# q's short-row loads on GpSimd's queue, the attention's steps for a pair laid singly, and k^T v two steps later in unit 2

## The chip, the cores and the metric

The kernel runs on one core of one Trainium2 chip. Its time is the device time of one launch in microseconds (us); the time before is a median of three runs. The profile is one further execution of the same program (span 956.1 us), recorded with its instructions, their waits and every DMA packet.

## The reference, cut to what matters

```python
# q, k, v: (8 batches, 8 heads, 576 rows, 64), float32
kv  = einsum('bhsd,bhse->bhde', k, v)            # k^T v, per batch and head
out = einsum('bhsd,bhde->bhse', q, kv)
rms = sqrt(mean(out * out, axis=-1) + 1e-6)
att = out / rms * g_norm                          # -> x: (4608 tokens, 512)
h = x @ w_in                                      # (4608, 2048)
r = maximum(h, 0)
y = (s * (r * r) + b) @ w_out                     # (4608, 512)
```

The attention is linear: all of k and v of a batch is folded into eight 64x64 matrices first, and each row of q only multiplies one of them. Nearly all arithmetic is in the two matrix products of the feed-forward block.

## The kernel before, in words

**Units and chunks.** The 4608 tokens are 36 chunks of 128 rows, and four chunks are a unit: nine units, `u = 0` to `8`, in one Python loop that is fully laid out. ("Unit 2" below is `u == 2`, the third of them.) A unit's feed-forward block has two parts. `mm1(u, s)` makes the hidden activations in four steps `s = 0..3`, each of seven products of a Strassen-like scheme, `x1, x3, z2, y4, x6, y7, x5` (`x3` and `y4` are those of the step before). `mm2(u)` multiplies by w_out; for `u > 1` it uses a second level of the same scheme, in the function `rest`, and its w_out blocks come from DRAM again for each unit.

**The order is written by hand** (`manual_schedule`): every engine executes its instructions in the order of the Python calls, and semaphores are put in where data need them. So an instruction that must wait holds up all that stands behind it on its engine, and a DMA that must wait holds up all DMAs behind it in the same issuing queue.

**Attention on the side.** While unit `u` is in its feed-forward block, the attention of unit `u + 1` is laid between its products by `sides(u)` (for `u = 0` and `1` by `side_of(u)`). Two pairs of chunks, A and B, pass through these steps: `turn` (VectorE transposes q), `product` (TensorE multiplies by k^T v, and VectorE turns the result back out of PSUM), `square` (ScalarE), `row_sum` (VectorE and a root on ScalarE), `norm` (VectorE), `turn_x` (VectorE), `scale` (ScalarE), and at the end `x_sums` (VectorE). The dictionary `first` maps a place `(s, n)` to the steps laid there: `n = 0` before `x1`, `1` after `z2` (and before `y4`), `2` after `x6`, `3` after `y7`. `second` holds places in `rest`, called by `at(...)`.

**k^T v.** `kv_product(b)` makes the matrices of batch b with 144 small matmuls. It reads k and v from four tiles of a ring of seven (`ringp`), which also carries all w_out blocks. `pump(k)` issues the next k loads of one long list (`queue_w2`) on SyncE's queue, lines L115 (k and v), L779 and L782 (w_out): a load waits until all that used the ring slot seven places earlier is done. In unit 1 the function `parts_of_w(i)` also writes second-level parts of w_out to DRAM: seven DMAs for each of six blocks, from GpSimd's queue (L826), three of them straight out of the ring tiles, so that those stores too must have landed before their slots can be loaded again.

**q.** A pair's q is one 128x1024 tile; the pool `qp` has two buffers, so a pair's load waits for the `norm` of the pair two before it. From chunk 9 on q is loaded by `load_q` in DMAs of one head and half of its 64 columns: 32 rows of n runs of 128 bytes, 16 DMAs for each contiguous stretch of the batch. In the kernel before all of them are issued from SyncE's queue, where the ring's loads are. The profile names them by the caller: L1341 in `loads`, which issues a whole pair, and L1352 in `loads_in_parts`, which spreads a pair over eight places of unit 1's second part. Output rows leave by GpSimd's queue (L914).

**parts.** `parts(c)` says which rows of which batch chunk c holds; `store` uses the same table, so any choice gives the same output. A chunk in the middle of a group of nine takes half its rows from each of two batches.

Of the kernel before, what the change touches and what calls it, by code (L numbers as in the profile page):

```python
# [16 lines left out]
def kernel(  # L17
# [39 lines left out]
    nc = tc.nc  # L57
    P = 128
    B, H, S, D = q.shape
# [10 lines left out]
    U = CH // 4  # L70
# [23 lines left out]
    kv_in, q_in, q_tile, w_raw = {}, {}, {}, {}  # L94
# [25 lines left out]
    def parts(c):  # L120

        g, i = divmod(c, R)
        n = 1 if g == 0 else 2
        if i == 4:
            return [(2 * g, 8 * n, n), (2 * g + 1, 8 * n, n)]
        b, i = (2 * g, i) if i < 4 else (2 * g + 1, i - 5)
        return [(b, i, 1), (b, 4 + i, 1)] if g == 0 else [(b, 4 * i, 4)]

    def load_q(c, queues=(nc.sync, nc.sync)):

        t = qp.tile([P, 2 * DM], FP32, name="q_sb", tag="q")
        q_tile[c] = t
        pieces = []
        for i in range(2):
            if c + i < R:
                q_in[c + i] = t[:, i * DM : i * DM + DM].rearrange("p (h d) -> p h d", h=H)
        for s, queue in enumerate(queues):
            for i in range(2):  # L140
                if c + i < R:
                    b, j, _ = parts(c + i)[s]
                    queue.dma_start(
                        out=q_in[c + i][s * HB : s * HB + HB],
                        in_=q[b].rearrange("h (p j) d -> p j h d", j=R)[:, j],
                    )
        for i in range(2):
            if c + i < R:
                continue
            w = 4 * i  # L150
            for b, j, n in parts(c + i):
                if pieces and pieces[-1][1] == b and pieces[-1][2] + pieces[-1][3] == j:
                    pieces[-1][3] += n
                else:
                    pieces.append([w, b, j, n])
                w += n
            q_in[c + i] = t.rearrange("p (a w) -> p a w", a=NP)[:, :, i * P : i * P + P]
            if c + i == R:
                q_in[R] = t[:, DM:].rearrange("p (a w) -> p a w", a=NP)
        rest = []  # L160
        for w, b, j, n in pieces:
            src = q[b].rearrange("h (t j) d -> h t j d", j=JC)
            to = t.rearrange("p (a w d) -> p a w d", a=NP, d=32)
            if c < R:
                to, w = t[:, DM:].rearrange("p (a w d) -> p a w d", a=NP, d=32), 0
            for h in range(H):
                for a in range(2):
                    rows = slice(32 * (2 * (h % 2) + a), 32 * (2 * (h % 2) + a) + 32)
                    rest.append(
                        partial(  # L170
                            nc.sync.dma_start,
                            out=to[rows, h // 2, w : w + n, :],
                            in_=src[h, :, j : j + n, a * 32 : a * 32 + 32],
                        )
                    )
        return rest
# [160 lines left out]
    for h in range(H):  # L337
        e = D // KC
        nc.gpsimd.dma_start(
            out=g_col[h * e : h * e + e, :], in_=g_norm.rearrange("(e c) -> e c", c=KC)  # L340
# [159 lines left out]
    def attention_of_two(c):  # L500
# [5 lines left out]
        u, j = divmod(c, 4)  # L506
        by_block = []
        for i in range(2):
            p = parts(c + i)
# [7 lines left out]
        W = 8  # L517
        st = {}
# [20 lines left out]
        def product():  # L539
            ps = [ps_t.tile([P, 2, 2 * P], FP32, name="y_ps", tag="t") for _ in range(2)]  # L540
            for b, lo, hi in runs:
                for r in range(2):
                    for p in range(NP):
                        for l in range(2):
                            rows = slice(l * HB, l * HB + HB)
                            at = l * HB + r * 32
                            nc.tensor.matmul(  # L547
                                ps[l][32 * p : 32 * p + 32, r, lo:hi],
                                lhsT=bd_kv[b % 2][rows, p, at : at + 32],
                                rhs=st["qT"][rows, p, lo:hi],  # L550
                                start=True,
                                stop=True,
                            )
            st["y"] = q_tile[c].rearrange("p (w l d) -> p w l d", w=W, l=2)
            for l in range(2):
                nc.vector.transpose(
                    out=st["y"][:, :, l].rearrange("p w (r e) -> p r w e", r=2),
                    in_=ps[l].rearrange("p r (w t) -> p r w t", w=W),
                )

        def square():
# [22 lines left out]
        def turn_x():  # L584
# [6 lines left out]
            )  # L591

        return dict(
            turn=turn, product=product, square=square, row_sum=row_sum, norm=norm,
            turn_x=turn_x, scale=lambda: scale_x(u, j),
        )

# [708 lines left out]
    def side_of(u):  # L1306

        A, B = pairs_of(u + 1)
        sums = lambda: [fn() for fn in x_sums(u + 1)]
        if u == 0:  # L1310
            side = {
                6: [lambda: kv_product(1)],
                7: [partial(A["turn"], 0), partial(A["turn"], 1)],
                8: [A["product"], A["square"]],
                9: [A["row_sum"], partial(B["turn"], 0), partial(B["turn"], 1)],
                10: [A["norm"], A["turn_x"], A["scale"], B["product"], B["square"]],
                11: [B["row_sum"], B["norm"]],
                12: [B["turn_x"], B["scale"], lambda: [fn() for fn in sums_w_in(0)]],
                13: [sums],
            }  # L1320
        else:
            side = {
                2: [partial(A["turn"], 0), partial(A["turn"], 1)],
                4: [A["product"], A["square"]],
                5: [A["row_sum"], B["turn"]],
                6: [A["norm"]],
                7: [A["turn_x"], A["scale"], B["product"], B["square"]],
                8: [B["row_sum"]],
                9: [B["norm"]],
                11: [B["turn_x"], B["scale"]],  # L1330
                12: [sums],
            }
            for n, fn in enumerate(loads_in_parts(3, 0, 8)):
                side.setdefault(6 + n, []).append(fn)
        return side

    def loads(u, i):

        if u < U:
            for load in load_q(4 * u + 2 * i):  # L1340
                load()  # L1341

    def loads_in_parts(u, i, parts):

        left = []

        def part(n):
            if n == 0 and u < U:
                left.extend(load_q(4 * u + 2 * i))
            k = -(-len(left) // (parts - n))  # L1350
            for load in left[:k]:
                load()  # L1352
            del left[:k]

        return [partial(part, n) for n in range(parts)]


    tile_at = {1: 3, 2: 4, 3: 5, 4: 6, 5: 7, 6: 8, 7: 9, 9: 10, 10: 11, 11: 12, 12: 13, 14: 14, 15: 15}
    more_at = {8: 8, 9: 9, 12: 10, 13: 11, 14: 12, 15: 13}
# [19 lines left out]
    def sides(u):  # L1379

        first, second = {}, {}
        if u + 1 < U:
            A, B = pairs_of(u + 1)
        kv = [lambda: kv_product(kv_due[u]), lambda: pump(NP)] if u in kv_due else []
        q = {half: [partial(loads, u + 2, half)] for half in range(2)}
        if u == 1:
            for s in range(1, NS):
                first[((0, 1), (0, 3), (1, 1))[s - 1]] = list(sums_w_in(s))  # L1390
            first[1, 3] = kv + [partial(loads, 2, 1)]
            return first, second
        if u + 1 == U:
            return first, second
        soon = u == 2
        first = {
            (0, 1): [A["turn"], *(kv if soon else [])],
            (0, 3): [A["product"]],
            (1, 0): [A["square"]],
            (1, 1): [*([] if soon else kv), A["row_sum"]],  # L1400
            (1, 2): [A["norm"], B["turn"]],
            (1, 3): q[0],
            (2, 0): [A["turn_x"], A["scale"]],
            (2, 1): [B["product"]],
            (2, 2): [B["square"]],
            (2, 3): [B["row_sum"]],
            (3, 0): [B["norm"]],
            (3, 1): [B["turn_x"], *q[1]],
            (3, 2): [B["scale"]],
        }  # L1410
        second[5], second[6] = [[lambda n=n: x_sums(u + 1)[n]()] for n in range(2)]
        return first, second

    for u in range(U):
        if u == 0:
            first_unit()
            second = mm2(0)
        else:
            if u < 3:
                loads(u + 1, u - 1)  # L1420
            steps = [mm1(u, s) for s in range(NS)]
            first, at_second = sides(u)
            second = mm2(u, steps[-1], at_second) if u > 1 else mm2(u)
# [81 lines left out]
```

## Time and profile before

| what | value |
|---|---|
| time before, median of 3 | 958.62 us (958.38 to 960.95) |
| profiled execution, span | 956.1 us |
| TensorE busy / VectorE / ScalarE / GpSimd | 922.4 / 670.8 / 197.0 / 87.8 us |
| DMA moved | 165.80 MB, mean 173 GB/s |
| q loads from SyncE with rows of 128 bytes | 304 DMAs |

TensorE is busy for 96% of the span. Its instructions overlap a little, so busy time alone doesn't say what is lost; the places where it stands still, and the clock that it is granted there, do. A table of stretches, one per unit, and the order of time on single engines are the views that answer that. In all of them "L" is the line of the kernel before, "SPq" and "POOL" are the queues of SyncE and GpSimd, and "idle before <-" names what ended an engine's wait.

### The profile page before, as it was taken

Reading aid. Unit: us, or ns where it says so; the run is one execution under the profiler, and the core shown is the slowest. Engines: PE = TensorE matmul, PEld = TensorE weight load, DVE = VectorE, ACT = ScalarE, POOL = GpSimd, SP = SyncE. Lnnn points to the kernel's source line nnn. Section 1 sums busy time; section 2 is a strip of 40 time slices with the busy share of each in tenths; the row PEclk is TensorE's granted clock in tenths of the full one; section 3 lists DMA queues with packets and bytes.
Section 4 is the critical chain, followed back from the end, with each engine's and each line's share of the span. In section 5 each row is a group of like instructions: output and inputs, shape, how many; then the busy total and the mean of one; then the engine's idle time right before and its main releaser. Section 6 shows DMA issues by size and latency. Waiting matters only on the chain.

```text
span 956.1 us, 17631 instructions
## 1 busy us (share of the span) xinstructions
PE 922.4 (96%) x7118; PEld 830.4 (87%) x7118; DVE 670.8 (70%) x1175; ACT 197.0 (21%) x355; POOL 87.8 (9%) x170
## 2 busy tenths in 40 slices
PE   7999999999589999979999999999999999999997
PEld 6888888888478998879988998899889988998897
DVE  2789777587357776765767776787587768774685
ACT  2684132101023102220123003300230023001200
POOL 2000010053300002000300020003000110011000
PEclk9999999999799999998999999999999999999999
DMA  9588837478852586137831784178516810682075
GB/s 234 197 315 242 268 90 207 113 237 289 256 150 38 172 257 226 24 83 240 267 104 23 266 274 134 21 232 261 178 29 204 285 61 1 201 286 65 12 229 168
DMA packets 129568, 165.80 MB, mean 173 GB/s; under 512 B 78160, under 2 KB 85072, under 8 KB 129360
## 3 DMA queue, kind: packets, MB, share of 16 engines
q1 hardware_dynamic: 118256, 142.71, 49.3%
q0 software_dynamic: 7488, 19.41, 6.1%
q10 hardware_dynamic: 3744, 2.56, 1.1%
q8 instruction: 56, 0.92, 0.4%
q14 instruction: 24, 0.20, 0.1%
HBM read 136.84 MB, written 27.79 MB: 172 GB/s over the span
## 4 chain that ended last, share of the span: by engine, by line
PE 81%; DVE 6%; SPq 6%; DMA 3%; ACT 3%; issue 1%; ACTq 0%; DVEq 0%
PE x_ps L91 36%; PE y_ps L91 25%; PE z_ps L91 9%; PE t_ps L91 8%; SPq L1341 2%; SPq L1352 2%; PE kv_ps L378 2%; DVE a L248 1%; PE y_ps L547 1%; DMA w_raw<-in_moe_w_in_dram 1%; ACT r L688 1%; SPq L115 1%; ACT xT L498 1%; DVE a L643 1%; DMA kv_sb<-in_k_dram 1%
## 5 line engine op out<-in xcount | busy, mean ns | idle before, releaser
L688 ACT COPY r<-x_ps 128x512 f32<-128x512 f32 x96 | 55.9, 583 | 466.4 <-PE x_ps L91 392.6
L91 PE MATMUL x_ps<-xs,ws 128*128 128x256 f32 x512 | 124.2, 386 | 2.2 <-ACT r L688 2.2
L91 PE MATMUL y_ps<-xs,wb 128*128 128x256 f32 x512 | 122.0, 381 | 0.0
L914 POOL DMA_DIRECT2D out_dram<-o x110 | 54.5, 502 | 711.3 <-DVE o L248 552.6
L91 PEld LDWEIGHTS x_ps<-xs,ws 128*128 128x128 f32 x512 | 96.8, 192 | 20.4 <-ACT r L688 4.6
L91 PEld LDWEIGHTS y_ps<-xs,wb 128*128 128x128 f32 x512 | 96.1, 190 | 14.5 <-issue 1.7
L91 PE MATMUL x_ps<-xT,wa 128*128 128x256 f32 x384 | 89.6, 380 | 0.1
L248 DVE TENSOR_TENSOR a<-y_ps,r 128x512 f32<-128x512 f32 x64 | 43.7, 683 | 59.8 <-ACT r L688 46.5
L91 PEld LDWEIGHTS x_ps<-xT,wa 128*128 128x128 f32 x384 | 72.3, 190 | 10.2 <-ACT xT L498 0.5
L91 PE MATMUL y_ps<-w_sb,sub 128*128 128x128 f32 x560 | 69.4, 275 | 0.0
L91 PEld LDWEIGHTS y_ps<-w_sb,sub 128*128 128x128 f32 x560 | 66.4, 192 | 0.4
L91 PE MATMUL x_ps<-w_sb,s 128*128 128x256 f32 x256 | 61.0, 394 | 5.7 <-DMA w_sb<-w 5.7
L643 DVE SCALAR_TENSOR_TENSOR a<-a 128x512 f32<-128x512 f32 x89 | 61.5, 691 | 2.8
L91 PE MATMUL y_ps<-w_sb,a 128*128 128x128 f32 (+1 forms) x416 | 61.0, 295 | 0.0
L91 PEld LDWEIGHTS x_ps<-w_sb,s 128*128 128x128 f32 x256 | 49.6, 199 | 13.0 <-issue 6.3
L91 PE MATMUL x_ps<-xT,ws 128*128 128x256 f32 x256 | 60.5, 379 | 0.0
L91 PE MATMUL z_ps<-xT,wa 128*128 128x256 f32 x256 | 60.5, 379 | 0.0
L91 PEld LDWEIGHTS y_ps<-w_sb,a 128*128 128x128 f32 x416 | 55.5, 192 | 2.0
L91 PE MATMUL t_ps<-w_sb,sub 128*128 128x128 f32 x448 | 54.6, 275 | 0.0
L91 PEld LDWEIGHTS z_ps<-xT,wa 128*128 128x128 f32 x256 | 48.6, 190 | 6.6
L91 PEld LDWEIGHTS x_ps<-xT,ws 128*128 128x128 f32 x256 | 48.1, 190 | 6.2
L91 PEld LDWEIGHTS t_ps<-w_sb,sub 128*128 128x128 f32 x448 | 52.3, 192 | 0.0
(159 smaller groups left out, 1357.3 us busy)
## 6 DMA issues: line engine op xcount, KB each, us to landing
w_sb<-w SPq DMA_DIRECT2D x154, 512.0 KB, 4.8
w_sb<-w SPq DMA_DIRECT2D x42, 256.0 KB, 3.6
w_raw<-in_moe_w_in_dram SPq DMA_DIRECT2D x8, 1024.0 KB, 7.7
w_raw<-in_moe_w_out_dram SPq DMA_DIRECT2D x8, 1024.0 KB, 5.3
w_sb<-in_k_dram SPq DMA_DIRECT2D x48, 144.0 KB, 3.6
w_sb<-in_v_dram SPq DMA_DIRECT2D x48, 144.0 KB, 4.0
w<-sub POOLq DMA_DIRECT2D x24, 256.0 KB, 5.6
out_dram<-o POOLq DMA_DIRECT2D x92, 64.0 KB, 4.4
```

Source lines behind the costliest of these rows:

```text
L91: nc.tensor.matmul(o, lhsT=lhsT, rhs=rhs, start=start, stop=stop, skip_group_check=True)
L115: nc.sync.dma_start(out=kv_in[b, n][r * HB : r * HB + HB, m], in_=src[b, NP * r + n].rearrange("(p j) d -> p j d", j=R),)
L248: nc.vector.tensor_tensor(out=o, in0=a, in1=b, op=ALU.add)
L378: nc.tensor.matmul(ps[r][l * HB : l * HB + HB, i, :], lhsT=kv[l][rows, 0, j, :], rhs=kv[l][rows, 1, j, :], start=(j == 0), stop=(j == R - 1),)
L498: nc.scalar.activation(to[:, i], to[:, i], AF.Copy, scale=g_col[:, i : i + 1])
L547: nc.tensor.matmul(ps[l][32 * p : 32 * p + 32, r, lo:hi], lhsT=bd_kv[b % 2][rows, p, at : at + 32], rhs=st["qT"][rows, p, lo:hi], start=Tr ...
L643: nc.vector.scalar_tensor_tensor(t, t, 0.0, t, ALU.max, ALU.mult)
L688: nc.scalar.copy(st[name], src)
L914: queues[s % 2].dma_start(out=view[b, jj, :, cols], in_=st[name, j][s * w : s * w + w, cols])
L1341: load()
L1352: load()
```

## The change

Three edits go together.

1. The DMAs of q in short rows are issued from GpSimd's queue. With that, `loads_in_parts` goes: in unit 1 the pairs of unit 2 are loaded whole at the start of the unit, and those of unit 3 whole after the two `norm` steps of its second part (places 6 and 9).
2. `product` is cut in two, `product` (TensorE) and `back` (VectorE's transposes out of PSUM), and the steps of both pairs are spread so that most places hold one. In unit 2 they stand later: `kv_product` goes from place (0, 1) to (1, 1), `product` of A from (0, 3) to (1, 3), and B's last steps move into `rest`.
3. `parts(c)` takes the rows of the middle chunk from the start of the second batch instead of its end, which makes some stretches contiguous: the pair at chunk 22 needs 32 DMAs instead of 48.

```diff
     def parts(c):
         g, i = divmod(c, R)
-        n = 1 if g == 0 else 2
+        if g == 0:
+            if i == 4:
+                return [(0, 8, 1), (1, 8, 1)]
+            b, i = (0, i) if i < 4 else (1, i - 5)
+            return [(b, i, 1), (b, 4 + i, 1)]
         if i == 4:
-            return [(2 * g, 8 * n, n), (2 * g + 1, 8 * n, n)]
-        b, i = (2 * g, i) if i < 4 else (2 * g + 1, i - 5)
-        return [(b, i, 1), (b, 4 + i, 1)] if g == 0 else [(b, 4 * i, 4)]
+            return [(2 * g, 16, 2), (2 * g + 1, 0, 2)]
+        return [(2 * g, 4 * i, 4)] if i < 4 else [(2 * g + 1, 4 * i - 18, 4)]
...
-                            nc.sync.dma_start,
+                            nc.gpsimd.dma_start,
                             out=to[rows, h // 2, w : w + n, :],
...
-            st["y"] = q_tile[c].rearrange("p (w l d) -> p w l d", w=W, l=2)
+            st["ps"] = ps
+
+        def back():
+            y = q_tile[c].rearrange("p (w l d) -> p w l d", w=W, l=2)
             for l in range(2):
                 nc.vector.transpose(
...
-                6: [A["norm"]],
+                6: [A["norm"], partial(loads, 3, 0)],
...
-                9: [B["norm"]],
+                9: [B["norm"], partial(loads, 3, 1)],
...
-            for n, fn in enumerate(loads_in_parts(3, 0, 8)):
-                side.setdefault(6 + n, []).append(fn)
...
-            first[1, 3] = kv + [partial(loads, 2, 1)]
+            first[1, 3] = kv
...
-        soon = u == 2
-        first = {
-            (0, 1): [A["turn"], *(kv if soon else [])],
-            (0, 3): [A["product"]],
-            (1, 0): [A["square"]],
-            (1, 1): [*([] if soon else kv), A["row_sum"]],
-            (1, 2): [A["norm"], B["turn"]],
-            (1, 3): q[0],
-            (2, 0): [A["turn_x"], A["scale"]],
-            (2, 1): [B["product"]],
-            (2, 2): [B["square"]],
-            (2, 3): [B["row_sum"]],
-            (3, 0): [B["norm"]],
-            (3, 1): [B["turn_x"], *q[1]],
-            (3, 2): [B["scale"]],
-        }
+        if u == 2:
+            first = {
+                (0, 2): [A["turn"]],
+                (1, 1): kv,
+                (1, 3): [A["product"]],
+                (2, 0): [A["back"]],
+                (2, 1): [A["square"]],
+                (2, 2): [A["row_sum"], B["turn"]],
+                (2, 3): [B["product"]],
+                (3, 0): [B["back"]],
+                (3, 1): [A["norm"]],
+                (3, 2): [A["turn_x"], *q[0]],
+                (3, 3): [B["square"]],
+            }
+            second = {
+                0: [A["scale"]], 3: [B["row_sum"]], "norm": [B["norm"]],
+                4: [B["turn_x"], B["scale"], *q[1]],
+            }
+        else:
+            first = {
+                (0, 2): [A["turn"]],
+                (0, 3): [A["product"]],
+                (1, 0): [A["back"]],
+                (1, 1): [A["square"], *kv],
+                (1, 2): [A["row_sum"]],
+                (1, 3): [B["turn"]],
+                (2, 0): [A["norm"]],
+                (2, 1): [B["product"], *q[0]],
+                (2, 2): [A["turn_x"], B["back"]],
+                (2, 3): [B["square"]],
+                (3, 0): [A["scale"], B["row_sum"]],
+                (3, 1): [B["norm"]],
+                (3, 2): [B["turn_x"], *q[1]],
+            }
+            second = {0: [B["scale"]]}
...
-            if u < 3:
-                loads(u + 1, u - 1)
+            if u == 1:
+                loads(2, 0)
+                loads(2, 1)
```

More of the change, by code (lines that the diff above doesn't have):

```diff
@@ L553, in product @@
                             )
-            st["y"] = q_tile[c].rearrange("p (w l d) -> p w l d", w=W, l=2)
+            st["ps"] = ps
+        def back():
+            y = q_tile[c].rearrange("p (w l d) -> p w l d", w=W, l=2)
             for l in range(2):
                 nc.vector.transpose(
-                    out=st["y"][:, :, l].rearrange("p w (r e) -> p r w e", r=2),
-                    in_=ps[l].rearrange("p r (w t) -> p r w t", w=W),
+                    out=y[:, :, l].rearrange("p w (r e) -> p r w e", r=2),
+                    in_=st["ps"][l].rearrange("p r (w t) -> p r w t", w=W),
                 )
@@ L593, in attention_of_two @@
         return dict(
-            turn=turn, product=product, square=square, row_sum=row_sum, norm=norm,
+            turn=turn, product=product, back=back, square=square, row_sum=row_sum, norm=norm,
             turn_x=turn_x, scale=lambda: scale_x(u, j),
@@ L1313, in side_of @@
                 7: [partial(A["turn"], 0), partial(A["turn"], 1)],
-                8: [A["product"], A["square"]],
+                8: [A["product"], A["back"], A["square"]],
                 9: [A["row_sum"], partial(B["turn"], 0), partial(B["turn"], 1)],
-                10: [A["norm"], A["turn_x"], A["scale"], B["product"], B["square"]],
+                10: [A["norm"], A["turn_x"], A["scale"], B["product"], B["back"], B["square"]],
                 11: [B["row_sum"], B["norm"]],
@@ L1323, in side_of @@
                 2: [partial(A["turn"], 0), partial(A["turn"], 1)],
-                4: [A["product"], A["square"]],
+                4: [A["product"], A["back"], A["square"]],
                 5: [A["row_sum"], B["turn"]],
-                6: [A["norm"]],
-                7: [A["turn_x"], A["scale"], B["product"], B["square"]],
+                6: [A["norm"], partial(loads, 3, 0)],
+                7: [A["turn_x"], A["scale"], B["product"], B["back"], B["square"]],
                 8: [B["row_sum"]],
-                9: [B["norm"]],
+                9: [B["norm"], partial(loads, 3, 1)],
                 11: [B["turn_x"], B["scale"]],
@@ L1341, in loads @@
                 load()
[L1343 to L1355, printed above, removed]
     tile_at = {1: 3, 2: 4, 3: 5, 4: 6, 5: 7, 6: 8, 7: 9, 9: 10, 10: 11, 11: 12, 12: 13, 14: 14, 15: 15}
```

## The prediction

> **What bounds the kernel now.** I read the page's first two parts, then a table of stretches cut at each unit's first matmul, then the order of time on TensorE where a unit is longer than its neighbours, then on SyncE's queue just ahead of it.
>
> ```profile
> PE 922.4 (96%) x7118; PEld 830.4 (87%) x7118; DVE 670.8 (70%) x1175; ACT 197.0 (21%) x355; POOL 87.8 (9%) x170
> ```
>
> TensorE is the bound, and little is left outside it. The stretches of units 2 to 6 (columns: length, then busy time of PE, PEld, DVE, ACT, POOL, granted clock, DMA share, GB/s):
>
> ```profile
> 243.13:358.53 115.40, 102.09 (x834) 92.56 (x833) 73.92 (x134) 17.83 (x35) 7.28 (x13) 0.94 0.58 167
> 358.53:466.11 107.58, 101.44 (x801) 91.42 (x801) 73.10 (x134) 17.84 (x35) 6.90 (x14) 0.97 0.51 158
> 466.11:564.72 98.61, 98.34 (x834) 89.60 (x833) 73.02 (x134) 17.84 (x35) 6.54 (x14) 1.00 0.55 167
> 564.72:663.32 98.60, 98.23 (x833) 89.59 (x833) 73.01 (x134) 17.84 (x35) 9.17 (x19) 1.00 0.56 169
> 663.32:761.92 98.60, 98.34 (x833) 89.78 (x833) 73.00 (x134) 17.84 (x35) 7.83 (x16) 1.00 0.57 173
> ```
>
> With the same work, units 4 to 6 take 98.60 us, unit 2 takes 115.40 and unit 3 107.58. The excess, 16.8 + 9.0 = 25.8 us, comes with a clock below 1.00. TensorE in order of time (start, length, and in brackets the idle time before):
>
> ```profile
> 246.67 1.37 PE L378 MATMUL kv_ps<-w_sb 64*64 64x64 f32 x74
> 249.16 0.30 PE L378 MATMUL kv_ps<-w_sb 64*64 64x64 f32 x2 [1.12 <-DMA w_sb<-in_v_dram]
> 257.81 0.47 PE L378 MATMUL kv_ps<-w_sb 64*64 64x64 f32 x2 [8.35 <-DMA w_sb<-in_v_dram]
> 259.08 2.15 PE L378 MATMUL kv_ps<-w_sb 64*64 64x64 f32 x66 [0.80 <-DMA w_sb<-in_v_dram]
> 261.16 3.68 PE L91 MATMUL x_ps<-xs,ws 128*128 128x256 f32 x8
> 269.19 1.36 PE L547 MATMUL y_ps<-qT,bd_kv 64*32 64x192 f32 x64 [2.62 <-DVE qT L526]
> ...
> 429.13 6.73 PE L91 MATMUL x_ps<-w_sb,s 128*128 128x256 f32 x16 [5.71 <-DMA w_sb<-w]
> ```
>
> Unit 2: `kv_product` runs from 246.67 to 261.16, 14.5 us where its row elsewhere takes 2.5: 12.0 lost. The next eight matmuls take 3.5 us to the next start, not 1.73: 1.8 lost. Then 2.62 us for q's transpose. Together 16.4. Unit 3: 5.71 us for a w_out block, then 16 matmuls in 6.73 us where the same row takes 3.46 elsewhere: 9.0. Each time SyncE's queue was busy with q:
>
> ```profile
> 242.64 11.01 SPq L1352 DMA_DIRECT2D q_sb<-in_q_dram  x8
> 253.81 1.11 SPq L115 DMA_DIRECT2D w_sb<-in_k_dram  x2
> 254.97 1.23 SPq L115 DMA_DIRECT2D w_sb<-in_v_dram  x2
> ...
> 380.93 43.50 SPq L1341 DMA_DIRECT2D q_sb<-in_q_dram  x64
> 424.54 0.38 SPq L779 DMA_DIRECT2D w_sb<-w  x1
> ```
>
> The last k and v tile of unit 2 was issued only at 253.81, behind eight q loads; in unit 3 no w_out block was issued for 43.5 us, behind 64 of them; units 4 and 5, with 48 q loads in 36.4 and 35.2 us, lost nothing. So it is the length of the block in SyncE's queue, against the time until the ring runs dry, that decides.
>
> **What the Trainium skill says.** "DMA: Bandwidth & Descriptors", section Issuing engines are not separate DMA queues: issuing from several engines "will only save the time on the sequencer". The trace agrees on what that can be worth: those 64 DMAs move 1 MB in 43.5 us, so the queue was the limit there, not the DMA engines. "TensorE: Matmul & The Clock Gate", section What's actually happening: after an idle window of about 3.4 us the clock is halved. The trace agrees (5.71 us idle, then 6.73 for 3.46). "Perfetto Trace Analysis", section DMA Instruction — SWDGE (GPSIMD): the recorded end of a GpSimd DMA is its last descriptor, not the data. The trace agrees: L826's stores take 0.546 us and land 5.6 us after issue. "SBUF — State Buffer", section Who interferes with whom: VectorE's copies in the two-port mode lock GpSimd out; unit 1 has none in the stretch below, and L826's stores take 540 to 555 ns beside VectorE's busy stretches as elsewhere.
>
> **The change part by part.**
>
> *Unit 3.* Its q loads leave SyncE, so the block for `x5_of(0)` is issued when its slot is free, as in unit 4. `parts` takes 16 of 64 DMAs away. Removes 9.0 us. On GpSimd 48 loads at 0.6 us are 29 us of a queue that has nothing else until the stores at the unit's end. Hidden. The same for units 4 to 7, where no wait was lost to this.
>
> *Unit 2, the price.* GpSimd now has a queue in unit 1 that matters. In order: `parts_of_w(7)`, 32 loads for chunk 12, 16 for chunk 14 (after B's `norm`, done at 231.9), two output stores, `parts_of_w(3)`. The last k and v tile of unit 2 takes the ring slot of block (3, 0), whose first store out of the ring is the first DMA of `parts_of_w(3)`. That this kind of wait binds shows at 227.80: SyncE waits 1.8 us for such a store with the first of the four tiles. So behind the 48 loads stands that store, behind it the tile, behind that TensorE. The trace has no q load on GpSimd. Nearest rows there: 502 ns (L914, 32 rows), 546 (L826 from sub, 128 rows), 764 (L826 out of the ring, 512 runs of 512 bytes), a slope of about 0.57 ns per run. The loads have 192, 64 and 256 runs: 0.59, 0.52 and 0.63 us, 16 of each, 27.8 us. Lower end 0.50 each, 24.0. Upper end 0.76 each, 36.5, by the 764 ns row; I also get about that if loads land in 6 us (as SyncE's did at 222 to 232) and eight are in flight, which is how the kernel's ninth GpSimd DMA, 2.80 us held for the first one's landing, reads.
>
> From the trace: GpSimd ends `parts_of_w(7)` at 223.0; +1.6, as the first loads wait for those stores to land; +27.8; +1.06 for two output stores; +0.76 for the ring store; +3.3 to land (the median of L826 at 193 to 200, a quiet stretch; about 6 in a busy one). That is 257.5. The tile needed 5.3 us from issue to the matmul before (253.81 to 259.08): ready at 262.8. TensorE comes to the place later than before: (1, 1) is after eight products, 243.13 + 8 x 1.73 = 257.0, and the first half of `kv_product` takes 1.25: 258.2. Wait: 4.6 us, and being over the idle window, 3.3 us at half clock as in unit 3. So 16.4 goes and 7.9 comes. The 2.62 us for q's transpose goes: q of chunk 12 is issued by about 243, and `turn` comes at (0, 2), about 248.
>
> *Laid singly.* In units 2 to 7 TensorE waits once each, 0.3 to 0.4 us (2.2 in all), for ScalarE's copy r, which waits for VectorE's add, which stands behind the transposes out of PSUM at (2, 1), 1.31 us. Now `back` stands after `y4`'s add. But at (3, 1) a `norm` of 1.46 us stands before that add where a transpose of 1.24 stood, with about 0.2 us to spare. I take half: 1.1 gained. In unit 2's `rest` VectorE gets 1.22 + 1.46 + 1.24 us more, in a stretch where it is busy about 18.6 of 23.2 us: it fits, nearly; 0.7 lost, between 0 and 2.
>
> *Units 0 and 1, the tail.* The order on TensorE stays. Unit 1 starts with 32 loads on GpSimd, from 144 to about 163, wanted at 195 and 216: hidden. Nothing moves in unit 8.
>
> Sum: 958.6 - 16.4 + 7.9 - 9.0 - 1.1 + 0.7 = 940.7.
>
> **The rivals.** (a) No wait is left in unit 2: at 0.50 us a load and landing in 3.3, the store lands at 253.7 and the tile is ready at 259.0, a wait under 1 us and no halved clock. For it: L914's short stores do 0.50. Against: more runs per DMA cost more in L826. 958.6 - 16.4 - 9.0 - 1.1 + 0.7 = 932.8. (b) GpSimd's pace is 0.76 and the store lands in 6 us: 223.0 + 1.6 + 36.5 + 1.8 + 6 = 268.9, ready 274.2, wait 16.0, clock 3.3: 952.1; unit 3 alone pays. For it: DMA share was 0.98 until 230. Against: SyncE no longer fills the DMA queues with q at the same time. (c) Slower: 128-byte runs cost GpSimd 1.1 us a load, which nothing in the trace bounds directly: 52.8 us, ready near 290.5, wait 32.3: 968.4. Against: 512 runs cost 0.76.
>
> **How the numbers follow.** A wait of a few us, forecast: 0.50. (a) 0.28. (b) 0.12. (c) 0.07, and 0.03 for values between (b) and (c), within 0.3% of before. Slower is (c) and a tail in `rest`: 0.08. Same 0.03, faster 0.89. The range goes from (a)'s bottom, with all 2.2 us of the copies gained, 931, to (b), 953.
>
> **What would show it.** Right: unit 3 at 98.6 us or a little less, no wait of TensorE for w_sb<-w; q_sb loads at POOL of 0.52 to 0.63 us; the first L826 store of block 3 issued at about 254; `kv_product` in unit 2 split by a single wait of about 5 us, then matmuls at twice their time. Wrong: that store before 251 (then (a)), loads over 0.7 us (then (b)), a wait of TensorE on VectorE in unit 2's `rest` above 2 us, or a wait for w_out left in unit 3.

## The result, and the profile after

| | us |
|---|---|
| before, median of 4 | 958.50 (958.17 to 960.95) |
| changed, median of 4 | 950.91 (949.44 to 953.23) |
| ratio, 95% interval | 0.9918 (0.9889 to 0.9946) |
| forecast | 940.7 (931 to 953) |

The change gains 7.6 us where 17.9 were forecast: the right direction, less than half of the size. The page's first line of engines, and the same table of stretches as before, units 2 to 6 (length, then busy time of PE, PEld, DVE, ACT, POOL, clock, DMA share, GB/s):

```profile
PE 920.6 (97%) x7118; PEld 828.4 (87%) x7118; DVE 668.6 (71%) x1175; ACT 197.6 (21%) x355; POOL 249.2 (26%) x458
```

```profile
241.43:354.68 113.25, 101.94 (x833) 92.13 (x832) 72.90 (x133) 18.14 (x35) 42.01 (x73) 0.95 0.58 182
354.68:454.12 99.44, 98.44 (x803) 89.31 (x801) 72.80 (x133) 17.95 (x35) 36.29 (x68) 1.00 0.56 169
454.12:553.71 99.59, 98.60 (x834) 89.70 (x833) 72.79 (x133) 17.93 (x35) 34.42 (x64) 1.00 0.54 168
553.71:653.21 99.50, 98.50 (x835) 89.71 (x833) 72.80 (x133) 17.95 (x35) 34.43 (x64) 1.00 0.53 167
653.21:752.84 99.63, 98.64 (x835) 89.93 (x833) 72.80 (x133) 17.93 (x35) 26.26 (x48) 1.00 0.54 170
```

Read against the stretches of before: unit 3 lost 8.1 us of its 9.0 of excess and its clock is back at 1.00. Unit 2 lost only 2.1 of 16.8, and its clock is still low. Units 4 to 6 became longer, by 0.9 to 1.0 us each. Unit 7 (752.84 to 849.58) takes 96.7 where it took 95.9. The start of unit 2 is 1.7 us earlier, all of it before unit 1 begins; the profiles below put that start between 240.2 and 243.1 in seven kernels that leave unit 0 alone and load no more on SyncE in unit 1, so this is scatter and not the change.

Unit 2 on TensorE in order of time (start, length, idle before):

```profile
255.33 1.38 PE L381 MATMUL kv_ps<-w_sb 64*64 64x64 f32 x76
264.80 0.44 PE L381 MATMUL kv_ps<-w_sb 64*64 64x64 f32 x2 [8.09 <-DMA w_sb<-in_v_dram]
265.86 2.15 PE L381 MATMUL kv_ps<-w_sb 64*64 64x64 f32 x66 [0.62 <-DMA w_sb<-in_v_dram]
267.94 3.15 PE L91 MATMUL y_ps<-xs,wb 128*128 128x256 f32 x8
...
289.01 1.10 PE L550 MATMUL y_ps<-qT,bd_kv 64*32 64x256 f32 x32 [0.99 <-DVE qT L529]
```

The wait for the last v tile is there as forecast, but 8.7 us long and not 4.6. The two queues that lead to it, GpSimd's and then SyncE's:

```profile
240.22 12.38 POOL L1345 DMA_DIRECT2D q_sb<-in_q_dram  x22 [0.96 <-DMA q_sb<-in_q_dram]
252.59 1.08 POOL L920 DMA_DIRECT2D out_dram<-o  x2
253.67 1.55 POOL L832 DMA_DIRECT2D w<-w_sb  x2
255.21 1.63 POOL L832 DMA_DIRECT2D w<-sub  x3
```

```profile
256.74 1.10 SPq L115 DMA_DIRECT2D w_sb<-in_k_dram  x2
257.88 3.29 SPq L115 DMA_DIRECT2D w_sb<-in_v_dram  x2
262.72 12.04 SPq L785 DMA_DIRECT2D w_sb<-w  x7
```

The chain is the forecast one: q loads to 252.6, two output stores, the first store of block 3 at 253.67, and when it has landed the tile, at 256.74. But then the two v loads take 1.6 us each to issue where they took 0.594 before, and the tile is complete 9.1 us after its issue began (256.74 to 265.86), not 5.3. From 260 to 268, after the 8.09 us of idling, the granted clock is 0.50 to 0.51: the 66 matmuls take 2.15 us and the eight behind them 3.15, where they take 1.23 and 2.00 in experiment 1.

### The profile page after: what moved, and what is told of

Same layout as the page of the kernel before. It is cut to its first block, busy times and chain, and to the rows that moved or that the text cites. A ratio compares the mean times of both kernels' runs of the same rounds, so it can differ in the third digit from the quotient of the medians.

```text
span 948.0 us, 17626 instructions
## 1 busy us (share of the span) xinstructions
PE 920.6 (97%) x7118; PEld 828.4 (87%) x7118; DVE 668.6 (71%) x1175; ACT 197.6 (21%) x355; POOL 249.2 (26%) x458
## 2 busy tenths in 40 slices
DMA packets 78624, 165.80 MB, mean 175 GB/s; under 512 B 22608, under 2 KB 31824, under 8 KB 78416
## 5 line engine op out<-in xcount | busy, mean ns | idle before, releaser
L1345 POOL DMA_DIRECT2D q_sb<-in_q_dram x288 | 161.2, 568 | 204.2 <-issue 111.8
L920 POOL DMA_DIRECT2D out_dram<-o x110 | 54.7, 504 | 361.2 <-DVE o L251 214.4
L91 PEld LDWEIGHTS y_ps<-xs,wb 128*128 128x128 f32 x512 | 96.7, 192 | 18.8 <-DVE a L251 4.3
L91 PEld LDWEIGHTS x_ps<-xT,wa 128*128 128x128 f32 x384 | 72.3, 190 | 10.2 <-ACT xT L501 0.5
L91 PE MATMUL x_ps<-w_sb,s 128*128 128x256 f32 x256 | 57.8, 380 | 0.0
```

The lines of the kernel that those rows point to most:

```text
L91: nc.tensor.matmul(o, lhsT=lhsT, rhs=rhs, start=start, stop=stop, skip_group_check=True)
L920: queues[s % 2].dma_start(out=view[b, jj, :, cols], in_=st[name, j][s * w : s * w + w, cols])
```

## The experiments

All are timed beside the kernel before, in three rounds (the last in five). Their ratios are to the kernel before, with the 95% interval in brackets.

**1. Chunk 14's loads behind the stores.**

```diff
-                9: [B["norm"], partial(loads, 3, 1)],
+                9: [B["norm"]],
...
-                12: [sums],
+                12: [sums, partial(loads, 3, 1)],
```

> The changed kernel with one edit: in unit 1 the 16 loads of chunk 14's pair stand behind the stores of w_out blocks 3 and 4 in GpSimd's queue, not ahead of them. Theory 1 (GpSimd's order delays the store that frees the ring slot, and with it the last k and v tile): the first store of block 3 is issued some 9 us earlier (16 loads of 0.57 us), about 245 in place of 253.7; the tile is issued near 248 and, even if it takes 9 us as it did, is there at 257, when TensorE comes to it: wait under 1 us, unit 2 about 101 to 102 us in place of 113.3, the whole about 940. Theory 2 (the DMA engines are full there, so that the tile is late wherever its issue stands): the tile takes longer the earlier it is issued, the wait stays above 4 us, the whole above 946.

940.69 us (939.18 to 941.21), ratio 0.983 (0.979 to 0.987). Unit 2 takes 104.07 us. TensorE:

```profile
255.69 1.38 PE L381 MATMUL kv_ps<-w_sb 64*64 64x64 f32 x76
258.27 0.29 PE L381 MATMUL kv_ps<-w_sb 64*64 64x64 f32 x2 [1.19 <-DMA w_sb<-in_v_dram]
259.12 1.23 PE L381 MATMUL kv_ps<-w_sb 64*64 64x64 f32 x66 [0.55 <-DMA w_sb<-in_v_dram]
260.27 2.00 PE L91 MATMUL y_ps<-xs,wb 128*128 128x256 f32 x8
```

Theory 1 holds: 16 loads in front of one store made 9 us of unit 2. The wait is 1.7 us (I had put it under 1, and the unit at 101 to 102), and the matmuls after it run at full pace (2.00 for eight, not 3.15). The tile was issued at 249.54 and took 9.6 us, as slow as before; experiment 9 is about that.

**2. The steps of units 3 to 7 in their old places.**

```diff
-                (0, 2): [A["turn"]],
-                (0, 3): [A["product"]],
-                (1, 0): [A["back"]],
...
-                (3, 1): [B["norm"]],
-                (3, 2): [B["turn_x"], *q[1]],
...
+                (0, 1): [A["turn"]],
+                (0, 3): [A["product"], A["back"]],
...
+                (3, 0): [B["norm"]],
+                (3, 1): [B["turn_x"], *q[1]],
```

> The changed kernel with the attention's steps of units 3 to 7 where they were before (VectorE's turn back right behind the product, B's norm at (3, 0)); queue, rows and unit 2 as changed. Theory 1 (the new places cost: B's norm now stands right ahead of the add that frees r): units 3 to 6 go from 99.4 to 99.6 us back to 98.6, unit 7 from 96.7 to 96.1, in all about 4.5 us less, some 946.5. Theory 2 (the longer units come from GpSimd's loads beside VectorE, not from the places): units stay at 99.5, the whole at 951.

945.49 us (944.53 to 952.9), ratio 0.990 (0.985 to 0.995). Units 3 and 4:

```profile
353.84:452.53 98.69, 98.26 (x803) 89.32 (x802) 73.11 (x133) 17.84 (x35) 35.65 (x67) 1.00 0.55 171
452.53:551.17 98.64, 98.38 (x835) 89.68 (x833) 73.02 (x133) 17.83 (x35) 34.38 (x64) 1.00 0.55 168
```

The same loads on GpSimd (35 us of POOL), and the units are back at 98.6. So the longer units come from the places. What they do shows in step 3 of unit 4 of the changed kernel, all engines in order of time:

```profile
500.66 1.22 DVE L583 TENSOR_TENSOR xn<-q_sb,inv 128x1024 f32<-128x1024 f32 x1
...
501.80 0.68 DVE L251 TENSOR_TENSOR a<-y_ps,r 128x512 f32<-128x512 f32 x1
...
502.57 0.58 ACT L694 COPY r<-x_ps 128x512 f32<-128x512 f32 x1 [5.61 <-DVE a L251]
503.12 1.24 DVE L594 STREAM_TRANSPOSE xT<-xn 128x1024 f32<-128x1024 f32 x1
503.21 2.00 PE L91 MATMUL x_ps<-xs,ws 128*128 128x256 f32 x8 [0.46 <-ACT r L694]
...
507.52 1.99 PE L91 MATMUL y_ps<-xs,wb 128*128 128x256 f32 x8 [0.53 <-DVE a L251]
```

B's norm (500.66) stands ahead of y4's add (501.80), ScalarE's copy waits for that add and TensorE for the copy: 0.46 us. Then `turn_x` at 503.12 pushes the next adds back, and TensorE waits a second time, 0.53. The kernel before had one such wait in a unit, 0.3 to 0.4.

**3. The new rows alone.** The kernel before with the new `parts` only.

> The kernel before with the new choice of rows alone (parts), so that the block of q loads in SyncE's queue in unit 3 is 48 and not 64 DMAs; everything stays on SyncE. Theory 1 (what starves the ring in unit 3 is the length of that block; 48 fit, as units 4 and 5 show): unit 3 goes from 107.6 to 98.6, unit 2 stays at 115.4, the whole at about 949.5. Theory 2 (unit 3 needs the queue freed): the block is 33 us in place of 43.5 but the wait only shrinks, unit 3 over 102, the whole over 953.

948.02 us (946.71 to 948.37), ratio 0.991 (0.987 to 0.994). Units 2 and 3:

```profile
243.05:357.68 114.63, 101.96 (x833) 92.47 (x832) 73.77 (x133) 17.84 (x35) 7.64 (x14) 0.94 0.58 168
357.68:456.28 98.60, 98.17 (x802) 89.24 (x801) 73.01 (x133) 17.84 (x35) 6.90 (x14) 1.00 0.56 171
```

Theory 1 holds, for the places of before (experiment 6 shows that it needs them). Sixteen fewer DMAs give all 9 us of unit 3, on SyncE's queue. The smallest of the three edits by itself gains what all three together gain; the intervals can't tell the two apart.

**4. The queue alone.**

```diff
-                            nc.sync.dma_start,
+                            nc.gpsimd.dma_start,
```

> The kernel before with q's short-row loads on GpSimd's queue and nothing else: rows, steps, places and the eight parts of the pair of chunk 12 as before, so that four loads, not 48, come between two of w_out's block stores. Theory 1 (the order in GpSimd's queue decides unit 2): the first store of block 3 stands behind 16 loads, is issued near 236, the tile is there near 250, and k^T v at its old place (0, 1) waits 0 to 3 us where it waited 10.3; but the last of chunk 12's loads now stand behind block 4's stores and q's transpose comes late, by up to 6 us; unit 3 at 98.6. The whole 938 to 944. Theory 2 (GpSimd's loads are slow or collide with the stores wherever they stand): unit 2 as long as in the changed kernel, 113 us or more, the whole 948 or more.

949.81 us (949.32 to 951.3), ratio 0.993 (0.991 to 0.995). Unit 3 is at 98.6, unit 2 at 117.2:

```profile
247.01 1.23 PE L378 MATMUL kv_ps<-w_sb 64*64 64x64 f32 x66 [0.49 <-DMA w_sb<-in_v_dram]
...
267.15 2.13 PE L547 MATMUL y_ps<-qT,bd_kv 64*32 64x192 f32 x64 [15.26 <-DVE qT L526]
```

Theory 2's totals are met (113 or more, 948 or more), but not by its reason: the loads of chunk 12 issue in 0.57 us each (median), as in the changed kernel. Theory 1's order explains both halves of what is seen, and its total fails. k^T v, at its old place, waits 0.5 us where it waited 10.3: with 16 loads ahead of block 3's store and not 48, the tile comes in time. But the rest of chunk 12's loads now end behind block 4's stores, at 261.9, and q's transpose makes TensorE wait 15.3 us; I had put that at 6 or less. One queue holds both, and whichever stands behind pays.

**5. Experiment 1 with other places.** In units 3 to 7 the places of before, but `back` of B at (2, 2), after y4's add, and of A at (1, 0).

> The first experiment's order of loads, and in units 3 to 7 the places of before with one step moved: each turn back out of PSUM stands after the next add that frees r (B's at (2, 2), A's at (1, 0)) in place of right behind its product. Theory 1 (a wait for r comes from what stands ahead of y4's add on VectorE; before it was B's turn back, in the changed kernel it is B's norm): neither stands there now, both small waits are gone, units 3 to 6 at 98.2 to 98.4, unit 7 at 95.6, unit 2 at 104 as in the first experiment, the whole at 935. Theory 2 (VectorE is so full that a wait comes back somewhere): units at 98.6 or more, the whole at 936 or more.

935.64 us (935.03 to 936.22), ratio 0.977 (0.975 to 0.980). Units 3 to 6 take 98.4 to 98.6, unit 2 103.2. The waits of step 3 are gone and so is the old one of step 2: theory 1 holds for units 3 to 6, a little above its 98.2 to 98.4. Unit 7 takes 96.9, a miss: TensorE waits there 0.96 us for r in step 1, as theory 2 had it.

**6. All three edits, but q from SyncE.**

> The changed kernel with q's short-row loads on SyncE's queue again; rows, places and the whole pairs loaded at places 6 and 9 as changed. Theory 1 (one queue for another: the last k and v tile waits behind 48 loads in either): the loads of chunk 12 and the first three tiles end near 252, the 16 loads of chunk 14 near 261, the tile is issued there and ready near 267, a wait of about 10 us as in the changed kernel; unit 3 at 99.4 as its block is 48; the whole at 950 to 953. Theory 2 (GpSimd's queue is what frees the ring in unit 3 and what makes unit 2 better): unit 3 over 102, unit 2 over 118, the whole over 957.

964.47 us (961.88 to 967.49), ratio 1.008 (1.005 to 1.010): slower than before. Theory 2's bounds for unit 3 and the whole are met; both theories missed the main place. The tile's wait in unit 2 is gone; the loss is in unit 1, which takes 116.5 us and not 102.6, and in units 3 to 5 (104.9, 102.9, 102.1):

```profile
248.61 8.38 PE L91 MATMUL y_ps<-w_sb,a 128*128 128x256 f32 x24 [10.72 <-DMA w_sb<-w]
```

32 loads in one block at place 6 hold SyncE from 221.4 to 242.7, and the last w_out load of unit 1 stands behind them.

Unit 3 has the same 48 DMAs here as in experiment 3, and yet TensorE waits 3.51 us for w_out. The cause is hidden in the prediction's row of 43.50 us for the kernel before, because a view joins equal issues across a pause. The pause shows when the stretch is cut:

```profile
380.93 8.57 SPq L1341 DMA_DIRECT2D q_sb<-in_q_dram  x16
399.79 1.23 DVE L577 TENSOR_TENSOR xn<-q_sb,inv 128x1024 f32<-128x1024 f32 x1
401.08 23.36 SPq L1341 DMA_DIRECT2D q_sb<-in_q_dram  x48
```

For 11.6 of the 43.5 us the queue only stood and waited for B's `norm`, which frees the buffer of the second pair. So two things decide when the next w_out block can be issued: when that norm ends, and how many loads follow it. From the start of unit 3 to that issue it is 66.0 us in the kernel before (TensorE waits 5.71 us), 58.8 in experiments 3 and 8 (no such wait), and 64.8 here, where B's norm comes 5.0 us later. On SyncE's queue the 48 DMAs fit with the old places and not with the new ones.

So with the changed places and pairs loaded whole, the queue edit is worth some 14 us (964.5 against 950.9, from two sessions; 15 by the ratios).

**7. k^T v one place later.** Experiment 5, with k^T v at (1, 2) in unit 2 and B's transpose ahead of A's row sum.

> Experiment 5 with k^T v of unit 2 one more place later, at (1, 2), and B's transpose ahead of A's row sum at (2, 2). Theory 1 (the rest of the wait in unit 2 is the tile, ready at 259.1 where TensorE came at 256.7, and the 1.2 us of row sum ahead of the transpose): at (1, 2) TensorE comes 3.5 us later, the waits of 1.7 and 1.0 us go, unit 2 at 101 to 101.5, the whole at 932. Theory 2 (the copies of k^T v on ScalarE are then too late for A's product at (1, 3), one product further on): a new wait of 0.5 to 1.5 us there, the whole at 933 to 934.

934.48 us (934.09 to 937.12), ratio 0.977 (0.974 to 0.979). Both old waits go and a new one of 1.82 us comes in A's product, after 13 of its 64 matmuls; unit 2 stays at 103.1. The size is near theory 2's, but the profile shows no releaser for it, and ScalarE's copies had ended 0.7 us before the first of these matmuls. Its cause stays open. By the times, 935.03 to 936.22 there and 934.09 to 937.12 here, the two kernels can't be told apart.

**8. Experiment 5 with q from SyncE.**

> Experiment 5 with q's short-row loads on SyncE's queue again, so that of the queue edit nothing is left; chunk 14's 16 loads stand behind the last k and v tile there. Theory 1 (order and length in a queue matter, not which engine issues): the last tile is issued near 254, after 32 loads and three tiles, and is ready in 5 to 6 us, as block 3's stores have landed by then: ready at 259 to 260, a wait of 2 to 4 us and perhaps some of the halved clock; unit 2 at 103 to 106, the whole at 934 to 937, as experiment 5 or a little slower. Theory 2 (SyncE's 32 loads are slow beside block 7's stores, as in the kernel before, where eight took 11 us): the tile not before 265, the whole over 941.

947.17 us (946.21 to 948.78), ratio 0.990 (0.987 to 0.992). Theory 1 falls, with its total. Theory 2's total is met, but not its place: the tile is issued at 250.39 and k^T v runs without a wait. Unit 2 takes 102.0 and units 3 to 6 98.4, but unit 1 takes 115.2: the same w_out load stands behind the same 32 loads (TensorE idle 10.29 us). I had asked about the tile, and not about what else stands behind the block.

**9. The store first, then the loads.** Experiment 5, with chunk 14's loads right behind block 3's first store, and B's transpose ahead of A's row sum.

```diff
                 nc.gpsimd.dma_start(out=w3_dram[i][:, n], in_=t)
+                if i == 3 and n == 0:
+                    loads(3, 1)
```

> Experiment 5 with chunk 14's 16 loads placed between the first store of w_out block 3 (the one that frees the ring slot) and its other six, and B's transpose ahead of A's row sum at (2, 2) in unit 2. Theory 1 (the last k and v tile took 9.1 us from issue in the changed kernel and 9.6 in the first experiment, in place of 5.3 before, because the other stores of blocks 3 and 4 are in the DMA engines beside it): now only light loads are beside it, so that it is ready 5 to 6 us after its issue, near 253 to 254 on experiment 5's axis, and TensorE, there at 257, doesn't wait; the transpose's wait of 1.0 us goes too: unit 2 at 100.5 to 101.2 in place of 103.2, the whole at 933. Theory 2 (a tile issued alone, after a pause of SyncE's queue, takes 9 us whatever is beside it): ready not before 256.5, some of the wait stays.

933.47 us (932.46 to 935.03), ratio 0.977 (0.975 to 0.979). By the ratios, experiments 5, 7 and 9 can't be told apart; what decides between the theories is the trace. SyncE, then TensorE, then unit 2 as a stretch:

```profile
247.43 1.12 SPq L115 DMA_DIRECT2D w_sb<-in_k_dram  x2
248.59 1.23 SPq L115 DMA_DIRECT2D w_sb<-in_v_dram  x2
261.70 12.04 SPq L785 DMA_DIRECT2D w_sb<-w  x7
```

```profile
255.58 2.56 PE L381 MATMUL kv_ps<-w_sb 64*64 64x64 f32 x144
```

```profile
241.67:342.59 100.92, 99.31 (x834) 90.12 (x832) 72.88 (x133) 18.14 (x35) 42.32 (x74) 1.00 0.66 204
```

Theory 1 holds. The tile's v loads issue in 0.594 us again and land in 3.4 and 3.6: complete 5.4 us after the issue began. Theory 2 falls, as the queue had paused here too. k^T v runs in one piece, unit 2's clock is 1.00, and it takes 100.9 us. At 248 to 252 the DMA share is 0.78; in experiment 5, with the stores beside the tile, it is 0.98.

## Why the prediction was wrong, point by point

- **Unit 3, "Removes 9.0 us".** Right; the clock came back too. With the old places either edit suffices, fewer DMAs (experiment 3) or the queue (experiment 4); with the new places the queue edit is needed (experiment 6). The reading "the queue was the limit there" is half right: for 11.6 of the 43.5 us the queue waited for B's norm. The unit ended at 99.4 and not 98.6 for its places (experiment 2).
- **GpSimd's order as the new wait in unit 2.** Right, shown by experiments 1 and 9. Its terms held: 0.568 us a load against 0.58 forecast, the store's landing 3.1 us against 3.3. The tile was issued at 256.7; the forecast 257.5 lies at 255.8 on this profile's axis, 0.9 us earlier.
- **"The tile needed 5.3 us from issue to the matmul before": this step failed, a mis-sized term.** It measured 9.1. The 5.3 was read where the stores of w_out were over (the last had been issued at 248.80, and landed 0.6 us after the tile's issue began). I put the tile right behind the first of fourteen such stores and kept the quiet figure. Experiment 9 shows that these stores are the cause: with light loads beside the tile it takes 5.4. So the wait was 8.7 and not 4.6. The halved clock and the broken run cost about 2.7 besides (1.4 in k^T v, 1.3 in the matmuls after it), not 3.3. Together 11.4 against 7.9.
- **"I take half: 1.1 gained": this step failed, in its sign.** Laying singly cost 0.8 to 1.0 us a unit in units 3 to 7, some 4.5 in all. The text named the norm ahead of y4's add as the danger, with 0.2 us to spare, and only took half of the gain off for it. It didn't follow what `turn_x` at (3, 2) does one product later.
- **Unit 2's other terms.** The transpose of chunk 12's q no longer waits. B's now does, 0.99, with A's row sum ahead of it; I hadn't looked for it. In `rest` 1.6 us in three waits, against 0.7, within the stated 0 to 2.

The two failed steps, 3.5 and 5.6 us, and these last, 1.9, make 11.0 us; forecast and result are 10.2 apart.

The 950.9 us lie inside the stated range and close to rival (b)'s 952.1, but that is chance: (b) wanted 0.76 us a load on GpSimd and a store that lands in 6, and neither came.

## What to carry to other kernels

Moving transfers to another queue moves the waiting line there: list what now stands behind them, which buffer it frees, and who wants that buffer. Before moving anything, count the DMAs in each block and look for a wait inside it; with the old places a contiguous choice of rows, 16 fewer DMAs, did for unit 3 what the queue was moved for. Take the duration of a transfer from a moment with the same traffic beside it, and give every instruction ahead of the add that frees a buffer its price in that buffer's slack.

## What the runs showed of the hardware that was not expected

A load's own time on SyncE's queue is no constant: the same 144 KB loads of v took 0.594 us to issue in the kernel before and in experiment 9 (DMA share 0.63 to 0.82), and 1.57 to 1.68 in the changed kernel with GpSimd's stores in flight (0.96 to 1.02 from 256 to 264).

The same short rows make fewer packets from GpSimd's queue: with q moved, SyncE's queue lost 60160 packets and GpSimd's gained 9216 for the same 7.1 MB, some 118 and 770 bytes a packet (129568 in all became 78624). The two queues' share of DMA time hardly moved, 55.4% before and 54.7% after.

Neither SyncE's queue nor GpSimd's has more than eight DMAs under way. In all eleven traces a DMA starts only after the one eight places ahead in its queue has landed (on GpSimd at least 0.28 us after), while the one seven places ahead is at times still under way. The records show why: the program gives the DMAs of a queue eight semaphores in turn, and a DMA waits for the earlier use of its own.
